# Three tables give the 1262 tasks of an attention and feed-forward kernel another order, other engines and other buffers

## The chip, the core and the metric

The kernel runs on one core of a Trainium2 chip. The time is device microseconds (us) of one execution, the median of three runs. The engines that the document speaks of are PE (the matrix engine), DVE (VectorE), ACT (ScalarE), POOL (GpSimd) and the DMA queue of SP (SyncE). PSUM is what PE writes its products into; SBUF is the working memory. All engines run at once, each through its own list of instructions in order.

## The reference

```python
def attention(q, k, v):            # B=4, H=8, S=768, D=64
    scores = q @ k.T / sqrt(D)     # heads 0, 2, 6: causal
    ...                            # heads 1, 3, 4, 5, 7: causal, and only the first
                                   # 4 keys and the last 64
    return softmax(scores) @ v

x = attention(q, k, v)  as 3072 tokens x 512
g = x @ w_gate                     # 512 x 1536
silu = g * sigmoid(g)
out = (silu * (x @ w_val)) @ w_out # 1536 x 512
```

Inputs and outputs are 32-bit floats. The kernel computes in 16-bit floats and sums in 32 bits.

## The kernel before

The 3072 tokens are 24 tiles of 128, and six groups g0 to g5 of four tiles. The attention goes by tiles t0 to t23. For a tile, q and k come from DRAM, are cast to 16 bits (the buffer ring `hq`) and transposed on PE. `sc` tasks (L571) are the score products, 64 rows deep; ACT takes their exponential (`exps`, L583, into the ring `e`); a `mask` task (L591) multiplies the exponentials by zeros and ones; PE multiplies by the values (L601); a `norm` task on DVE (`nm`, L608 and L609) divides by the row sums; PE transposes (L625), which gives the columns of the group's `xt`.

The feed-forward goes by groups. For g0 and g1, gate and value products are plain (L763), 12 pieces of 128 hidden columns each. ACT takes the tanh (L769), DVE makes silu from it (`stt1`, L776) and multiplies by the value product (`stt2`, L790, into `h_sb`). From g2 on the value product, and for g4 and g5 the gate product too, is made from seven half-size block products (`w_product`, L1092) instead of eight. These need sums of weight blocks (`vw`, L1041) and of `xt` blocks (`xs`, L1072), copies of partial results from PSUM into SBUF (`wy`, L211 on ACT, L213 on DVE, into the ring `raw`), additions (`wa` and `wb`, L1113), silu on ACT (L1134), and the product of gate and value (`wh`, L1151 on POOL, L1154 on DVE, into `h_sb`). The output product of every group is made from seven block products as well (`seventh`, L845, tasks `out0.p1` to `out5.p7`). It needs sums of blocks of `h_sb` (`hs`, L815; `hs4.2.0` is sum 2 of group 4, first half) and of the output weights (`ws`, L416). Its seventh product p3 needs sum 4. The results are gathered in `out_sb` (`oe`, L889 and L213) and stored by a DMA.

Rings are small sets of buffers. `raw` has 11 buffers of 4 KB a partition, and serves loads, the `wy` copies and some sums; `e` has 6, `xb` 3, `sil` 3. PSUM has 8 `banks`. A task that takes a buffer waits until the last users of the one that stood in it are done. At the very start ACT (or DVE) fills the mask patterns (`mfill`, L288) once.

All this is written as tasks: each has a name, the engines it may run on, what it depends on, and the rings it takes from. Nothing decides the order at build time but three tables of numbers. `ORDER` is a list of 1262 two-character numbers in base 62: the sequence in which the tasks are emitted, and each engine and each DMA queue runs its own tasks in that sequence. `WAYS` has a digit for each task: which of its possible engines runs it. `SLOTS` has a digit for each buffer that is taken: which buffer of the ring, or which PSUM bank. Two lines give the choices that the prediction speaks of most: a copy or sum has its engine from the table, and `wh` on POOL is another instruction than `wh` on DVE.

```python
ENG[T_hs[g, x][part].way].tensor_tensor(out=to, in0=a, in1=b, op=op)   # hsum, L815
...
if T_wh[g, s, name].way == "POOL":
    nc.gpsimd.tensor_tensor(out=to, in0=w_cell("g", g, s, name),
                            in1=w_value("v", g, s, name), op=ALU.mult)
```

Of the kernel before, what the change touches and what calls it, by code (L numbers as in the profile page):

```python
# [21 lines left out]
    "3Z3f9h0l443G459j493g4A3a9k9l9q3n463c1F3H0L0r0K0M3h9r9m3o3dA73A3p3B3q3r9b9c3zA23e1G4H47A8A3A94N4K"
    "AA3sA54L4O4C4Q4R4DA4AB3t4ZA6AF484BAE4Y8eAG3w3xAHAkBJAnAl0N0u184e0P0v0O4g0x4f0s0SAmAoBEBM4E4FBTBH"
    "4dBKBL4M3y5DBFBO4GBNBGAzBWB9BU4cBV5CBPBIBQBXB04bBA4V8f4P8g4i4lBCAu4I1H1Q5g0t5K4hB14j1BBBBDAx4S4T"
    "Af4mAv12Aw8hAaB2Ai0w5L0R5J5n5I5o4WAgAy4UAh4q4oBR15Ab1E4r4p4v1K1I4n4aB3AjAcAp514yAq524z4k1M1R4sBS"
    "4tAr4u1S1O1JACAD545W5T555U5X5f5350AI1N8kAJB4AK5M56AO5Y8l1LAMAPAN0T0W0b4J4w57Ad580Q5H5E6M1P1T5h6L"
    "5G6K7P5N5k5FB55i0U6H6J5j59AQAs5AAeAR5cALAUB74x5l4X5BAtB6B8AVAS5v5V5OBb8iBw5p5s5w5qAW0V5m0X0Y5tCF"
    "C0BxAXC1C75P5QBz5RC8CG6IATCUCMC2CbCVDBCW5Z5aCHC3Cc6v8jBy5r5uCdC45b5dCXC5CYCB5x6wC9606O6P6N735S74"
    "CZAZCI72CNCC5yCaC6CQCDCeDCCJCKCA5z66CfCE67DJDFDK63CRCgDDDEBaBcCO64DG686165CSCLCP6EChD76RCTDLDMCi"
    "6SD8DHDID9DABY7F697G6ACvCwCz6Z6UCj6aBZD06B6CBdBeCxCy6D6eBfCk6VBg7C6XBk6YAY620a5e0d6Q0Z7H6TClCmD1"  # L30
    "DRD37DD4DS7L7O6W7E6zBiBlBh6FD2D5DTBm6y80Bn706G0e7X717WBj81Dt6bDN6cCrBoDOCsD66dDU6xCtDPCu6p6hBqBp"
    "6q6i6f7I7J7KBrCnCoDvDuDQCp0c7U896gERES6k75BsDxET6l766mBtCqDy6n7bDzE46oE07c776jE5DXDYE678EgE16rEU"
    "E26s79E3EVEY6tFK7A7QEhE7EZ7eEW7fDZEiEj7YDaEaDw0f857j88827BBu866u87Bv7N7VFLEcEdFMFOEwEeEkEXFP7Z7a"
    "EfFQElEb7RF0ECE8FNEmFR8m7T7d7M7SExEDF1EnE9EyEzF2EJF8DVDcDbEAEKELENEEF4F3EB7g7hDWF5EFF97iDd7mEGDh"
    "F67nEHF7Di7pEo7k7qEpEODeFAFBEPEIEMEQDjDk8oDg7x8q84EqEr8A8B7rFq8s7o8C8nDf7s8D8N837tDlDm8Q8R8YEsFC"
    "7u7v8Z8E7wDn8I8GDoFG8pFr8F8SFDEtEuEv7yFH8J8HDpG8GFFIFEFJFFG9FuGaGAGh8KGGFvGbDqFs8rFVG18L8MGiGjG2"
# [1332 lines left out]
```

## Time and profile before

| what | before |
|---|---|
| time, median of 3 runs | 237.11 us (236.71 to 237.15) |
| profiled execution, its time | 236.62 us |
| its span | 234.8 us |
| PE busy | 224.4 us, 96% |
| DVE busy | 208.3 us, 89% |
| ACT busy | 177.6 us, 76% |
| POOL busy | 162.9 us, 69% |
| granted clock of PE, mean | 0.998 |

The span goes from the first to the last instruction of the profiled execution; its time has 1.8 us more around it. The granted clock is in parts of the higher of PE's two levels, 2.4 GHz. A busy share is a mean over stages that are limited by different things.

### The profile page before, as it was taken

To read this page: it belongs to the slowest core of one execution; us is meant where nothing else is said; L and a number is where in the kernel's file an instruction comes from. 1 tells how busy PE (TensorE), PEld (TensorE's weight loads), DVE (VectorE), ACT (ScalarE), POOL (GpSimd) and SP (SyncE) were. 2 spreads that over 40 slices of the span, in tenths; PEclk is the share of its full clock that TensorE was granted. 3 is DMA by queue.
4 is the path that set the end of the run, shared out by engine and by line. 5 is a ranking of instruction groups with operands and counts; after the bars stand their busy time and mean duration, and the time that the engine had idled before them with its cause. 6 is when DMAs were issued, how large, how long until landed. Compare 5 with 4: busy or idle time off the path is not lost.

```text
span 234.8 us, 6223 instructions
## 1 busy us (share of the span) xinstructions
PE 224.4 (96%) x2418; PEld 165.9 (71%) x2418; DVE 208.3 (89%) x373; ACT 177.6 (76%) x294; POOL 162.9 (69%) x180
## 2 busy tenths in 40 slices
...
GB/s 177 334 360 349 349 366 330 310 255 271 323 324 145 286 203 250 153 170 209 209 170 145 112 139 178 4 0 25 24 146 80 3 0 92 41 49 3 36 147 179
DMA packets 67197, 40.77 MB, mean 174 GB/s; under 512 B 25184, under 2 KB 61024, under 8 KB 67168
## 3 DMA queue, kind: packets, MB, share of 16 engines
...
## 4 chain that ended last, share of the span: by engine, by line
PE 76%; DVE 11%; SPq 4%; issue 3%; DMA 2%; POOL 1%; ACT 1%; DVEq 0%; POOLq 0%; ACTq 0%
PE banks L845 23%; PE banks L1092 20%; PE banks L763 20%; PE banks L571 6%; PE banks L601 5%; SPq L353 3%; DMA raw<-in_k_dram 2%; DVE h_sb L790 2%; DVE sil L776 2%; DVE e L591 2%; POOL h_sb L1151 1%; PE banks L477 1%; SPq L358 1%; DVE xb L609 1%; DVE h_sb L1154 1%
## 5 line engine op out<-in xcount | busy, mean ns | idle before, releaser
L583 ACT ACTIVATE e<-banks 128x1024 f16<-128x1024 f32 (+2 forms) x68 | 59.6, 914 | 9.4 <-PE banks L571 8.4
L763 PE MATMUL banks<-xt,wg_sb 128*128 128x512 f16 (+1 forms) x208 | 48.4, 363 | 0.8 <-DVE h_sb L790 0.7
L211 ACT COPY raw<-banks 128x512 f32<-128x512 f32 x61 | 33.9, 589 | 17.8 <-PE banks L1092 8.9
L845 PEld LDWEIGHTS <-h_sb 128*128 128x128 f16 x420 | 40.4, 98 | 7.0 <-issue 0.4
L769 ACT ACTIVATE sig<-banks 128x512 f32<-128x512 f32 (+1 forms) x52 | 28.6, 567 | 6.4 <-PE banks L763 3.7
L763 PEld LDWEIGHTS <-wg_sb 128*128 128x128 f16 x208 | 18.7, 98 | 16.7 <-issue 1.2
L1113 DVE TENSOR_TENSOR raw<-banks,raw 128x512 f32<-128x512 f32 x36 | 24.0, 684 | 3.7 <-ACT raw L211 2.1
L815 POOL TENSOR_TENSOR h_sb<-h_sb 128x768 f16<-128x768 f16 x11 | 18.7, 1707 | 12.2 <-DVE hs_sb L815 7.2
L845 PE MATMUL banks<-wt_sb,h_sb 128*128 128x256 f16 x216 | 26.2, 273 | 0.0
L591 POOL TENSOR_TENSOR e<-e,m 128x640 f16<-128x640 f16 (+1 forms) x14 | 24.8, 1779 | 0.9 <-ACT e L583 0.6
L845 PE MATMUL banks<-wo_sb,h_sb 128*128 128x256 f16 x204 | 24.9, 273 | 0.3 <-DVE h_sb L790 0.3
L763 PE MATMUL banks<-xt,wv_sb 128*128 128x512 f16 (+1 forms) x112 | 24.6, 349 | 0.0
L213 POOL CAST vt<-raw 64x512 f16<-64x512 f32 x24 | 14.8, 620 | 13.1 <-DMA raw<-in_v_dram 12.3
L571 PEld LDWEIGHTS <-kT 64*128 64x128 f16 x472 | 14.5, 94 | 11.0 <-issue 10.0
L571 PE MATMUL banks<-qT,kT 64*128 64x128 f16 x472 | 21.2, 218 | 0.4 <-DVE kT L213 0.2
L1092 PE MATMUL banks<-raw 128*128 128x256 f16 x144 | 20.3, 273 | 0.6 <-ACT raw L211 0.6
L1092 PEld LDWEIGHTS <-raw 128*128 128x128 f16 x192 | 18.1, 98 | 3.8 <-issue 0.8
L601 PEld LDWEIGHTS <-e 128*128 128x128 f16 x472 | 17.6, 97 | 4.3 <-issue 1.1
L1113 POOL TENSOR_TENSOR raw<-raw 128x512 f32<-128x512 f32 x12 | 16.0, 1331 | 6.4 <-DVE raw L213 3.7
L601 PE MATMUL banks<-vt,e 128*128 128x65 f16 x472 | 18.8, 193 | 1.2 <-POOL vt L213 0.8
L609 DVE TENSOR_TENSOR xb<-banks,rc 128x512 f16<-128x512 f32 x24 | 16.6, 691 | 0.8
L776 DVE SCALAR_TENSOR_TENSOR sil<-sig,banks 128x512 f32<-128x512 f32 (+1 forms) x28 | 16.6, 606 | 0.5
...
## 6 DMA issues: line engine op xcount, KB each, us to landing
...
```

Of the source, the lines that this page charges most:

```text
L211: nc.scalar.copy(out=dst, in_=src)
L571: nc.tensor.matmul(sc[:, c:c + n, :], weights, moving, start=first, stop=last)
L583: nc.scalar.activation(out=to, in_=src, func=AF.Exp, scale=scale)
L591: ENG[task().way].tensor_tensor(out=ev, in0=ev, in1=mm, op=ALU.mult)
L601: nc.tensor.matmul(avs[t][:, odd, n * 66:n * 66 + 65], ee, vv, start=(m == 0), stop=(m == len(bl) - 1))
L609: nc.vector.tensor_tensor(out=xb.rearrange("p n o d -> p o n d"), in0=av[:, :, :, 0:64], in1=rc.to_broadcast([128, 2, 4, 64]), op=ALU.mult)
L763: nc.tensor.matmul(ps, wsb[:, kk, j * 128:(j + 1) * 128], xt[:, kk, c[0]:c[1]], start=(kk == 0), stop=(kk == 3))
L769: nc.scalar.activation(out=sg[g, j, c], in_=gs[g, j, c], func=AF.Tanh, scale=0.5)
L776: nc.vector.scalar_tensor_tensor(out=sl[g, j, c], in0=sg.pop((g, j, c)), scalar=1.0, op0=ALU.add, in1=gs.pop((g, j, c)), op1=ALU.mult)
L845: nc.tensor.matmul(rooms[g, p][:, x, lo:hi], left[:, j, 128 * x:128 * x + 128], right[:, j, lo:hi], start=(on is None and (j == 0 if apart ...
L1092: nc.tensor.matmul(w_rooms[on][:, m], right, left[:, kk], start=(begins and m == 0 and kk == 0), stop=(kk == 1), skip_group_check=True)
L1113: ENG[T_wc[mat, g, s, name].way].tensor_tensor(out=to, in0=other, in1=to, op=ALU.add)
```

## The change

The three tables are replaced. The 1262 tasks, their dependencies and the instructions that each engine form of a task issues are the same. About 170 tasks run on another engine than before, the emitting sequence differs nearly throughout, and buffers and banks are dealt anew. The packed work of each engine stays nearly what it was: the moves between DVE, ACT and POOL go both ways. The first lines of each table:

```diff
 ORDER = (
-    "0607090A08000201202122231Z1Y1b0B251a0C0D041U1V0h0n0G0g0m0E0k1W031c1d1X1f1g1i051j1e1h281p2B1r2W2X"
...
 WAYS = (
-    "000011000000000000000000000000000000000000000000000000000000012002202212202102021010000110010110"
...
+    "000010000000000000000000000000000000000000000000000000000000212022122202222201021010011011101020"
...
 SLOTS = (
-    "65879104218319647A8636400543570374730564275A9835971023532245002212163406011042020206340121372062"
...
+    "034201675A127053142756590A7125769265938984809A6390A467520634362314120602436062414034402031523461"
```

What the tables do is seen in the engines' lists. The first place is the start, ACT. `mfill` fills are the rows at L288 (m_101 to m_103 are mask patterns), the casts to `hq` are the first halves of q and k, and the first row at L583 is the exponential of tile 0. Before:

```order
L288 ACT_TABLE_LOAD
L288 ACTIVATE m_101<-nat 128x256 x2
L288 ACTIVATE m_101<-nat 128x384
L288 ACTIVATE m_101<-nat 128x128
L288 ACTIVATE m_103<-nat 128x384
L288 ACTIVATE m_103<-nat 128x128
L288 ACTIVATE m_102<-nat 128x256
L211 CAST hq<-raw 128x2x4x64 x2
L288 ACTIVATE m_103<-nat 128x128
L288 ACTIVATE m_102<-nat 128x256
L583 ACTIVATE e<-banks 128x1024 x6
```

The same place with the change:

```order
L211 ACT_TABLE_LOAD
L211 CAST hq<-raw 128x2x4x64 x2
L288 ACTIVATE m_101<-nat 128x256 x2
L288 ACTIVATE m_101<-nat 128x384
L288 ACTIVATE m_101<-nat 128x128
L288 ACTIVATE m_103<-nat 128x384
L288 ACTIVATE m_103<-nat 128x128
L288 ACTIVATE m_102<-nat 128x256
L211 COPY kT_104<-banks 128x512
L583 ACTIVATE e<-banks 128x1024 x2
```

The casts moved ahead of the fills; a copy of kT came to ACT ahead of the first exponential; the last two fills went to DVE.

The second place is the end of the stage in which attention tiles 9 to 11 run beside g0's feed-forward. On DVE the rows from the masks (L591) to the sum of value weights (L1041) stand around tile 10; `wt_sb` rows (L416) are `ws` sums. Before, from the mask of tile 10 on:

```order
L591 TENSOR_TENSOR e<-e,m_102 128x1024
L416 TENSOR_TENSOR wt_sb<-wo_sb 128x512
L416 TENSOR_TENSOR wt_sb<-wo_sb,wt_sb 128x512
L790 SCALAR_TENSOR_TENSOR h_sb<-sil,banks 128x512
L776 SCALAR_TENSOR_TENSOR sil<-sig,banks 128x512
L608 RECIPROCAL rc<-banks 128x8
L609 TENSOR_TENSOR xb<-banks,rc 128x2x4x64
```

With the change:

```order
L591 TENSOR_TENSOR e<-e,m_102 128x1024
L591 TENSOR_TENSOR e<-e,m_103 128x640
L416 TENSOR_TENSOR wt_sb<-wo_sb 128x512
L1041 TENSOR_TENSOR raw<-wv_sb 128x768
L776 SCALAR_TENSOR_TENSOR sil<-sig,banks 128x512 x2
L608 RECIPROCAL rc<-banks 128x8
L609 TENSOR_TENSOR xb<-banks,rc 128x2x4x64
```

The second mask of tile 10 and a weight sum came to DVE, one `ws` sum left. POOL at the same place before (`wo_sb` casts are output weights, `vt` casts values, `hq` casts q and k; m_103 is the pattern of the second mask of a tile):

```order
L213 CAST wo_sb<-raw 128x1024
L416 TENSOR_TENSOR wt_sb<-wo_sb 128x512
L213 CAST hq<-raw 128x2x8x64
L416 TENSOR_TENSOR wt_sb<-wo_sb 128x512 x2
L591 TENSOR_TENSOR e<-e,m_103 128x640
L213 CAST vt_110<-raw 64x2x2x2x64
L213 CAST hq<-raw 128x2x8x64
L213 CAST vt_109<-raw 64x2x2x2x64 x3
```

With the change:

```order
L815 TENSOR_TENSOR h_sb<-h_sb 128x3x256
L1041 TENSOR_TENSOR raw<-wv_sb,raw 128x768
L213 CAST wo_sb<-raw 128x1024
L416 TENSOR_TENSOR wt_sb<-wo_sb 128x512
L213 CAST wo_sb<-raw 128x1024 x2
L416 TENSOR_TENSOR wt_sb<-wo_sb 128x512 x2
L416 TENSOR_TENSOR wt_sb<-wo_sb,wt_sb 128x512 x2
L416 TENSOR_TENSOR wt_sb<-wo_sb 128x512
L815 TENSOR_TENSOR h_sb<-h_sb 128x3x256
```

The mask and the casts of q, k and v are no longer between the weight sums; casts and sums of weights, and `hs` sums, stand there one behind the other.

The third place is POOL from group 4's last `wh` tasks on. The rows at L1151 are `wh4.2.c11` alone and then `wh4.2.c22`, `wh4.2.c12` before; L815 into `h_sb` ahead of them are sums of group 3, L815 into `hs_sb` is `hs4.1.1`, and the two L815 rows behind it are `hs4.4.0` and `hs4.4.1`:

```order
L1151 TENSOR_TENSOR h_sb<-raw 128x2x256
L1072 TENSOR_TENSOR raw<-xt 128x512
L815 TENSOR_TENSOR h_sb<-h_sb 128x3x256 x2
L1113 TENSOR_TENSOR raw<-raw 128x512
L1151 TENSOR_TENSOR h_sb<-raw 128x2x256 x2
L1113 TENSOR_TENSOR raw<-raw 128x512
L815 TENSOR_TENSOR hs_sb<-h_sb 128x768
L815 TENSOR_TENSOR h_sb<-h_sb 128x3x256
L1113 TENSOR_TENSOR raw<-raw 128x512
L815 TENSOR_TENSOR h_sb<-h_sb 128x3x256
```

With the change the first three L1151 are `wh4.1.c11`, `wh4.1.c22`, `wh4.2.c11`; L815 into `hs_sb` are `hs4.1.0` and `hs4.1.1`; the two L1151 between them are `wh4.2.c22` and `wh5.0.c11`; the L815 rows behind are `hs4.3.1`, `hs4.2.1`, `hs4.2.0` and, last, `hs4.4.1`:

```order
L1151 TENSOR_TENSOR h_sb<-raw 128x2x256 x3
L1072 TENSOR_TENSOR raw<-xt,raw 128x512
L1072 TENSOR_TENSOR raw<-xt 128x512
L815 TENSOR_TENSOR hs_sb<-h_sb 128x768
L1151 TENSOR_TENSOR h_sb<-raw 128x2x256 x2
L815 TENSOR_TENSOR hs_sb<-h_sb 128x768
L815 TENSOR_TENSOR h_sb<-h_sb 128x3x256
L815 TENSOR_TENSOR h_sb<-hs_sb,h_sb 128x3x256 x2
L1113 TENSOR_TENSOR raw<-raw 128x512 x2
L1151 TENSOR_TENSOR h_sb<-raw 128x2x256
L1113 TENSOR_TENSOR raw<-raw 128x512
L1151 TENSOR_TENSOR h_sb<-raw 128x2x256
```

`wh4.2.c12` went to DVE, the sums of group 3 went to DVE, three sums of group 4 came from DVE to POOL, and `hs4.4.0` went the other way. The row of `hs4.4.1` follows directly behind this piece.

## Rows read from the trace of the kernel before

**Rows 1.** The page: busy time by engine, and the last chain by engine.

```profile
PE 224.4 (96%) x2418; PEld 165.9 (71%) x2418; DVE 208.3 (89%) x373; ACT 177.6 (76%) x294; POOL 162.9 (69%) x180
...
PE 76%; DVE 11%; SPq 4%; issue 3%; DMA 2%; POOL 1%; ACT 1%; DVEq 0%; POOLq 0%; ACTq 0%
```

**Rows 2.** PE's timeline: start, us, instruction, [idle before, who ended it].

```profile
60.64 1.02 PE L763 MATMUL banks<-xt,wg_sb 128*128 128x512 f16 x4 [0.74 <-DVE h_sb L790]
73.86 0.93 PE L601 MATMUL banks<-vt,e 128*128 128x65 f16 x25 [0.28 <-DVE e L591]
75.13 1.47 PE L845 MATMUL banks<-wo_sb,h_sb 128*128 128x256 f16 x12 [0.34 <-DVE h_sb L790]
...
200.81 1.19 PE L1092 MATMUL banks<-xt,wv_sb 128*128 128x256 f16 x8 [0.83 <-DVE raw L213]
203.47 0.60 PE L1092 MATMUL banks<-raw 128*128 128x256 f16 x4 [0.59 <-ACT raw L211]
```

**Rows 3.** The chain of waits, 77 to 82 us: start, us, what.

```profile
78.34 1.31 PE banks L845 x12
...
80.20 1.42 PE banks L845 x12
```

**Rows 4.** ACT's timeline at the start.

```profile
4.33 2.25 ACT L288 ACTIVATE m<-nat 128x256 f16<-128x256 f16 x7 [2.30 <-POOL nat L264]
6.48 1.12 ACT L211 CAST hq<-raw 128x512 f16<-128x512 f32 x2
...
9.32 1.02 ACT L583 ACTIVATE e<-banks 128x1024 f16<-128x1024 f32 x1 [1.19 <-PE banks L571]
```

**Rows 5.** DVE's timeline: three long instructions, and a mask of the usual length.

```profile
57.08 2.06 DVE L591 TENSOR_TENSOR e<-e,m 128x1024 f16<-128x1024 f16 x1
67.59 1.40 DVE L1041 TENSOR_TENSOR raw<-wv_sb,raw 128x768 f16<-128x768 f16 x1
72.74 1.07 DVE L591 TENSOR_TENSOR e<-e,m 128x1024 f16<-128x1024 f16 x1
...
90.00 0.68 DVE L591 TENSOR_TENSOR e<-e,m 128x1024 f16<-128x1024 f16 x1
```

**Rows 6.** Groups by line and shape, DVE: busy, mean ns, idle before.

```profile
L1041 DVE TENSOR_TENSOR vt<-wg_sb,kT 128x768 f16<-128x768 f16 x2 | 1.1, 550 | 0.0
```

**Rows 7.** POOL's timeline at the middle place.

```profile
56.96 1.65 POOL L1041 TENSOR_TENSOR raw<-wv_sb 128x768 f16<-128x768 f16 x1
...
83.45 0.61 POOL L213 CAST vt<-raw 64x512 f16<-64x512 f32 x1 [10.19 <-DMA raw<-in_v_dram]
```

**Rows 8.** Windows: PE, PEld, DVE, ACT, POOL busy (counts), clock, DMA share, GB/s.

```profile
60.00:70.00 10.00, 9.36 (x76) 4.69 (x76) 9.65 (x15) 8.95 (x14) 8.57 (x10) 1.00 1.14 331
```

**Rows 9.** The chain of waits, 196 to 203 us.

```profile
196.92 0.54 ACT raw L1134
...
197.53 2.52 POOL h_sb L1151 x2
...
200.08 0.59 ACT raw L211
...
200.68 2.06 DVE h_sb L1154 x2
```

**Rows 10.** DVE's and POOL's timelines, 200 to 203 us.

```profile
201.27 1.45 DVE L1154 SCALAR_TENSOR_TENSOR h_sb<-raw 128x512 f16<-128x512 f32 x1
200.90 1.27 POOL L1113 TENSOR_TENSOR raw<-raw 128x512 f32<-128x512 f32 x1 [0.87 <-DVE raw L213]
```

**Rows 11.** The tail: the window from 206 us, POOL's timeline, PE's.

```profile
206.00:231.60 25.60, 25.57 (x235) 22.68 (x232) 21.18 (x36) 10.84 (x21) 13.17 (x9) 1.00 0.19 66
...
209.06 1.64 POOL L815 TENSOR_TENSOR h_sb<-h_sb 128x768 f16<-128x768 f16 x1 [4.83 <-DVE h_sb L1154]
211.88 1.65 POOL L815 TENSOR_TENSOR h_sb<-h_sb 128x768 f16<-128x768 f16 x1
...
219.19 2.78 PE L845 MATMUL banks<-wo_sb,h_sb 128*128 128x256 f16 x24
```

More of the change, by code (lines that the diff above doesn't have):

```diff
@@ L22 @@
[L22 to L36, printed above, removed]
@@ new lines @@
+    "0J0o0I0p9Y9d353S3T193E3Q173u3F369e9Z399vA0379w9fA19a3v3l3W9n0l0M0r0P0K0L3m3X3i3U9o9p2T3f9i3V3j3Y"
+    "3Z439g40443a3g3H41459h1A3k3h3c9b3n469l3o429j3d3A9q3e471G1F3G9cA7494A4Z9k3B9m9r3p4H3qA24K3rA8A9A3"
+    "3sA5AA3tA4A6AB4LAu4C4N4Q3y4D4MAF488eBJ4OAvAxAwBKBLAy4Y5D4B3w0u4g0N5L0x4R185KAkB9BMAl0O0t0v4e0s4h"
+    "0S4f4P4dAE1H1S3zAH8g1BBNAmBOAn3x4EBTBP4bBAAoBQBB4FBC4GAz5CBU4VB04cBDBV1Q15121I1K1R0w5I0W5J0Q0R4J"
+    "B1BWBEBFBX4o4l4i4p4j4aBHAfBG4IBI4vAg4mAp4S4TB2BRAq4W5g1EAh4UB3ArBSAi514y4q4r52AaAbB4B54zAj4k4n1M"
@@ new lines @@
+    "8fAc1N1O4s4tACB64u501PAG1J545T5WAIAJAD6J5H5UAKAdAsAOAM4w555f5X5FAPALAeAt8i531T1L5YAN8h0X5n0U4x5l"
+    "0b565M570T4X6M585NAQ5G6KAR6L5O59B75c5AB8AU5v5s5pAS5VAV5w5t5q5B0V6H5E5m0Y5o5j5kBw7P60ATAW5P5Q5ZCF"
+    "CUCMAX5RC7C0Cb8jBx5r8kBy5uBz8l6v5h5iCGCVCNCHCWDB5aC1CcCXC86ICYCfC25d5b5x5yDCC3CZCaC4CgChCB6wC5CI"
+    "5z66CdCOC967726N5S6P7374CCCiDDC6CJCD63CQCKCeCL64CACP61Bb6EBd6568DFCECRCS696RD7DGDECTDHDIDJCz6SD8"
+    "6A7F6ZD9DKD06a7GDACvDR6B7C6CDLD1CwDSDMD2DTCx6DCyBYDNAZ7D6X6UAY710a7O0Z625e0e6G6O6Q0dBZ6Y6V6FDO6T"
@@ new lines @@
+    "BaBg7HBcBeBfDU6zD3DPBkCrD46yCsD5DQD66W7LBj6bCj6cBq817E6f70DtDuCkBl6e6xBmBnCtBh6dClCu6p6h6iCnCmBr"
+    "Dx7I7J7KCo806qDyBo756k766lBpBiCpBsDzERE0Cq887U7W0f6g7N0c6n7bE4DvDX6jBt6m8mDZE5777cEYE1EgESE2ET6o"
+    "E378796r6s827ADwE6EZEUEh7R6tEwEV7Y7eE7Ei7TEjEW7f7Z8nEa84F0EXEcEJE8ECF1EbDY7X7B87897VBv6u86BuEdF2"
+    "EkFKEeExEyF3E985ElEmEzFLEAF4F8EnFMF5F6Ef7a7SDVEDEKF9EEEF7MFAEBFBFNF7ENFOEoEpEqEGDdEHFPDW7dDa7Q8q"
+    "DcELEI7g7hEM7jDbEODe7iDh7m7pEPDiDjFQErDgEQ7xDf8o7n7qDk7s8D8ADl7t8BDmFRFC8p8s7o7rFDFE8C7kFqFr8N8Y"
@@ new lines @@
+    "8QDn8Z7u7v8E838R8FDo7wFGEsFHFI8I8GDpFt7yFJFF8J8HDqEtEu8rFuGhGaFv8tFsGbGFFw8KG8GiG9G1GGG2EvFx8L8M"
+    "GcGAFy8T8WFzGdGB8UG4GeGf8XGCGkG5GlGDG0G6GIGmGEGoGvGgFVGJGK8SG3GHGjHIHOHKFXGnHJ7lDr7zDs8PHGG7GpHM"
+    "GwHLGLHHFSFZHNFUFWFY8VHUFaGqGrGMGyGTGsGNGOH2H9GtFTGUFeGzH3FbHA8OGVGuGxHBFfHP8aFk8bH0H4HQHSHRHTH5"
+    "GP8cH1HVGQGWH6FgHCGRH7HYHZ8dFdFcGXHDI2FhI3FlGSH8GYHWHXHEIDI6I7HFGZImInHaI5I4HgHbFmI8IoFiFnI9IpIE"
+    "HcHdIFIAIqIBIGItIuJUIKIwIRICIHIIILJSIrIMJ0IUIsHiIvFjIxIyJVFoHeISIzJTJ1FpINHhHjHlHkJ7IOIPHfIJJ8J2"
```

55 lines of the change are left out of this document (25 added, 30 removed).

## The prediction

> **What bounds the kernel now.** I read the page first, for busy time and for the last chain: PE works 224.4 of 234.8 us, DVE 208.3, and the chain that ended last is 76% PE and 11% DVE [rows 1]. So the end moves in two ways only: PE is given less to do, or one of its pauses goes or comes. The change has the same tasks, so the first way is nearly shut, and I went through PE's timeline for pauses behind another engine. Behind the start there are two places where PE waits in earnest [rows 2]. The reader is to see who ends each wait. In the middle, 60 to 75 us, it is DVE three times: 0.74 + 0.28 + 0.34 = 1.36 us. Late, at 200 to 204 us, it is a copy from PSUM to `raw`, once on DVE and once on ACT: 0.83 + 0.59 = 1.42 us. Then I read, for each place, the timelines of DVE and POOL and the chain of waits, to see why the releaser was late.
>
> In the middle DVE is full (9.65 of 10 us) while POOL works 8.57 [rows 8]. Three DVE instructions are much longer than their like [rows 5, 6]: a mask 2.06 us where another took 0.68, a sum of value weights 1.40 where 0.55 is usual, another mask 1.07. All three have two inputs in SBUF, and the first lies over a POOL sum that began at 56.96 and took 1.65 us [rows 7]. The excess is 1.38 + 0.85 + 0.39 = 2.62 us. That is more than the 1.36 us PE waits, so without the holds DVE would have been in time. Instructions of DVE that read one operand from PSUM keep their length over the same POOL work.
>
> Late, the chain of waits reads backward like this [rows 9]: PE's second pause ends with an ACT copy at 202.83, which needs a `raw` buffer that two DVE products (`wh5.0`) free; they need 2.06 us, because one of them is 1.45 us long beside a POOL addition [rows 10]. They stood behind a DVE copy that, like the ACT copy at 200.08, waited for a `raw` buffer; that buffer was freed by `wh4.2.c22` and `wh4.2.c12`, both on POOL, 2.52 us from 197.53 [rows 9]. These waited for ACT's silu at 196.92 and stood one behind the other.
>
> **The change part by part.** The sum is made against the profiled execution (236.62 us, span 234.8 and 1.8 around it); it is 0.49 below the median of 237.11, and I carry the difference over to the median.
>
> *PE's own work.* The same matmuls run. A row of output products behind score products took 1.42 us and one behind other work 1.31 [rows 3], so each entry into the 64-row scores costs about 0.1 us (an estimate from this pair). In the order of PE's list the scores stand in 36 separate groups before and 35 with the change: 0.1 us less; between 0 and −0.2.
>
> *Start.* Before, the fills (2.25 us) come first on ACT, then the casts (1.12), and the first exponential begins at 9.32 [rows 4]. With the change the casts come first, which lets PE begin earlier, but 2.25 us of fills and a copy then stand between the casts and the first exponential: I get it at about 10.1, 0.8 later. In exchange the second tile's q and k come earlier and ACT has less left after. PE's work up to the first gate product is limited by loads and DVE as well, so I put 0; bounds −0.4 (PE starts that much earlier and keeps it) and +0.8 (the whole delay of the exponential reaches PE).
>
> *Middle.* DVE's two-input instructions from 52 us to the last of the three waits are 7 before and 8 with the change: the second mask of tile 10 and a sum of value weights come, one sum of output weights goes. POOL's list there loses the mask and the casts of q, k and v that wait for loads (it waited 10.19 us for one [rows 7]) and becomes a row of casts and sums of weights without a pause. Nothing here tells which instructions will meet, since which of the two starts first decides. Per instruction the excess before was 2.62 / 7 = 0.37; eight of them make 3.0, so +0.4 us, which goes through to PE since DVE has no slack here. Lower bound: nothing is held and the 1.36 us of waits go, −1.4. Upper bound: five of eight held by the mean of the three long ones, 2.62 / 3 = 0.87, make 4.35, so +1.7.
>
> Read beside this: the Trainium skill, "SBUF — State Buffer", section "Who interferes with whom", says that DVE and GpSimd share one pair of ports as an exclusive lock, that a DVE instruction with two SBUF inputs contends with a GpSimd instruction that reads SBUF, and that the one issued first keeps it for its whole length. Rows 5 and 7 agree. By the rule, with POOL busy 0.86 of the stretch, nearly every one of the eight would meet an occupied port; half a POOL instruction of 1.2 us each makes about 0.5 x 8 = 4.1 us, an estimate, and the sum would come out 1.1 us higher than mine, 237.5 us. What hangs on it is the first rival, which is priced from rows alone.
>
> *Late.* `wh4.2.c12` leaves POOL for DVE, so that it no longer stands behind `wh4.2.c22`; the two group 3 sums and the addition that stood ahead of them on POOL are gone; and more PE work stands between the product that the late copies follow and the one that needs them. Each of these alone gives the copy at 200.08 its buffer about 1.3 us earlier (one POOL product of the pair that takes 2.52), enough for the pause of 0.83; the second pause of 0.59 hung on the first, through DVE's list. So −1.4. On DVE `wh4.2.c12` costs 0.68 us or 1.45 when held [rows 10]; behind it in DVE's list are additions of the same group that free PSUM banks, and DVE waited for POOL here before, so there is room. Bound: 0, if the buffers are dealt so that the wait stands elsewhere.
>
> *Tail.* From 206 us on PE has no pause (25.57 of 25.60 busy) and POOL works only 13.17 [rows 11]. POOL then waited 4.83 us before `hs4.4.0` and ended `hs4.4.1` at 211.88 + 1.65 = 213.53, 5.7 us ahead of the output product at 219.19 that needs both [rows 11]. The change gives POOL, from `hs4.1.1` to `hs4.4.1`, five sums of 1.65 us and five products or additions of 1.27 [rows 10, 11]: 14.6 us without a pause, so from about 202.1 to 216.7, while the output product comes 1.4 earlier, at 217.8. That leaves 1.1 us, in which every hold by DVE and every wait for an input has to fit. I take +0.4 (one hold of the size above and a little waiting use up 1.5 of the 1.1); bounds 0 and +1.5.
>
> The sum: −0.1 + 0 + 0.4 − 1.4 + 0.4 = −0.7 us. The profiled execution would take 235.9 us and the median 236.4.
>
> **The rivals.** *First, on the other side: DVE is held by POOL in the middle.* One mechanism, one place: at 52 to 77 us, five or more of the eight two-input instructions meet a POOL instruction. Then the middle term is +1.7 instead of +0.4, and the sum −0.1 + 1.7 − 1.4 + 0.4 = +0.6, a time of 237.7; with six held 238.6. It decides from an excess of about 3.7 us on (4.2 for a change that can be measured), against 2.62 now. For it: POOL's uninterrupted row of sums there, and DVE's 9.65 of 10 us. Against it: of seven only three were held, with POOL just as busy.
>
> *Second: the late wait only moves.* The eleven `raw` buffers are dealt anew, and the gaps between a copy and its reader are a few tenths there. If half of the 1.42 us returns at another product of g5, the sum is −0.1 + 0.4 − 0.7 + 0.4 = 0: 237.1. For it: DVE now has `wh4.2.c12` and the sums of group 3, ahead of copies that PE needs. Against: three things that made the wait are gone at once.
>
> *Third: the start is late.* The exponential's 0.8 us goes through, sum +0.1: 237.2. For it: nothing on ACT hides the fills any longer. Against: PE gets its first work earlier.
>
> *Fourth: more is won than I put.* No long hold in the middle and room in the tail: −0.1 − 1.4 − 1.4 = −2.9 at most, half of it likelier, 235.2.
>
> **How the numbers follow.** Forecast (late wait gone, the rest evens out, 235.6 to 236.6) 0.38; first rival 0.27; second 0.16; third 0.09; fourth 0.10. A difference under 0.2% (0.47 us) can hardly be told from none here. Faster: forecast and fourth, 0.48. Same: second and third, 0.25. Slower: the first, 0.27. The likeliest case gives 236.4. The range goes from 235.0 (half of the fourth case is below) to 238.2 (the first rival's five held, 237.7, and half of the way to six); some 0.15 lies outside.
>
> **What would show it.** Late: no wait of PE above 0.3 us between 196 and 205 us, and `wh4.2` on two engines. Middle: count DVE's masks and weight sums over 0.9 us between 50 and 78 us, and add what they have over 0.68 or 0.55; PE's waits behind DVE there should sum to about 1.8. Start: first exponential near 10.1, first gate product within 0.4 of where it was. Tail: `hs4.4.1` ending within 1.5 us of the output product that needs it, with a wait of a few tenths at the most. The forecast is wrong if the excess in the middle is above 3.7 us, if a wait for a `raw` buffer stands elsewhere after 195 us, or if PE waits for a sum on POOL at 210 to 222 us by more than 1 us.

## The result, and the profile after

The changed kernel takes 233.42 us (233.23 to 233.67), the kernel before 237.13 in the same comparison: a ratio of 0.9849 [0.9826, 0.9872], 3.7 us faster. The forecast was 236.4 with a range from 235.0 to 238.2. The sign was right, the size was not, and 233.42 lies outside the range. The profiled executions took 233.35 and 236.62 us. Medians and ratios leave out executions that took over 1.5% more than the fastest of the same kernel (one with the other kernel's order on SP, three with the early cast of k8).

The page of the changed kernel, busy time by engine; it answers to [rows 1]:

```profile
span 231.6 us, 6221 instructions
PE 223.0 (96%) x2418; PEld 165.6 (71%) x2418; DVE 205.4 (89%) x381; ACT 178.9 (77%) x295; POOL 160.3 (69%) x171
```

The matmuls are the same 2418. Of the 3.2 us between the spans, 1.8 are idle time of PE (8.6 instead of 10.4) and 1.4 its busy time, in which pauses can hide, since the ends of matmuls are modelled. Windows of the changed kernel (us, busy PE, PEld, DVE, ACT, POOL with counts, granted clock, DMA share, GB/s) at the two places of the prediction; they answer to [rows 2, 8]:

```profile
60.00:70.00 10.00, 10.00 (x96) 5.25 (x93) 9.70 (x20) 8.45 (x16) 9.78 (x9) 1.00 1.12 336
70.00:80.00 10.00, 10.00 (x116) 6.53 (x115) 9.76 (x20) 9.90 (x14) 6.27 (x6) 1.00 1.21 250
80.00:90.00 10.00, 10.00 (x142) 8.30 (x140) 9.84 (x22) 9.60 (x15) 6.81 (x9) 1.00 1.21 214
90.00:100.00 10.00, 10.00 (x116) 8.24 (x114) 9.79 (x21) 9.87 (x17) 6.14 (x8) 1.00 1.00 172
...
200.00:210.00 10.00, 10.00 (x94) 8.96 (x93) 7.92 (x14) 5.89 (x11) 8.27 (x6) 1.00 0.01 2
```

PE is busy for the whole 10 us in each of them; before it had 9.36 of 10 from 60 to 70 us [rows 8]. Of the five pauses in [rows 2] none is left. PE's timeline of the changed kernel has one pause above 0.3 us between 25 us and the last stage (0.35 at 32.69), and this one in the last stage:

```profile
214.64 1.47 PE L845 MATMUL banks<-wo_sb,h_sb 128*128 128x256 f16 x12
...
223.83 1.47 PE L845 MATMUL banks<-wt_sb,hs_sb 128*128 128x256 f16 x12 [0.29 <-DVE out_sb L889]
```

To see where time went although the tasks come in another order, I made an account from the two traces: for each PE task the time from its start to the next task's start, less the median of its kind over both traces, added up in order of time. It counts what PE lost, shown as a pause or not, and pauses come out larger than their rows (0.83 as 0.99, 0.59 as 0.75), for the same reason.

| change of the account from before to after | us |
|---|---|
| up to 50 us | +0.6 |
| 50 to 80 us | -2.1 |
| 80 to 100 us | -0.2 |
| 100 to 190 us, many small ones | -0.6 |
| 190 to 210 us | -1.9 |
| 210 us to the last product | +0.5 |
| sum | -3.7 |

Behind the last product 0.4 us more pass (3.6 instead of 3.3 to the end of the span), which makes, to rounding, the 3.2 us between the spans.

DVE in the middle of the changed kernel, two-input instructions; they answer to [rows 5, 6]:

```profile
52.91 0.69 DVE L591 TENSOR_TENSOR e<-e,m 128x1024 f16<-128x1024 f16 x1
54.58 0.56 DVE L1041 TENSOR_TENSOR raw<-wv_sb 128x768 f16<-128x768 f16 x1
...
72.32 1.14 DVE L591 TENSOR_TENSOR e<-e,m 128x1024 f16<-128x1024 f16 x2
73.72 0.55 DVE L1041 TENSOR_TENSOR raw<-wv_sb 128x768 f16<-128x768 f16 x1
```

All have their usual length (two masks of 0.68 and 0.48 in 1.14). None of DVE's ten such instructions from 52 to 77 us was held by 0.1 us or more. One reason is DVE's own list: from 55.2 to 72.3 us, where POOL works nearly without a pause (9.78 of 10 us in the window above), it has none of the ten. Before, the two longest stood in that stretch, at 57.08 and 67.59 [rows 5]. POOL's timeline gives the other reason; it answers to [rows 7]:

```profile
54.73 1.66 POOL L591 TENSOR_TENSOR e<-e,m 128x640 f16<-128x640 f16 x1 [3.23 <-ACT e L583]
73.94 1.35 POOL L416 TENSOR_TENSOR wt_sb<-wo_sb,wt_sb 128x512 f16<-128x512 f16 x1 [1.43 <-DVE wt_sb L416]
```

POOL stood still for 3.23 us, waiting for an exponential, while DVE did its masks at 52.9 to 54.7; and for 1.43 us, waiting for a sum on DVE itself, while DVE did its row at 72.3 to 73.7.

### The profile page after: what moved, and what is told of

It reads as the page before. It is cut to its first block, busy times and chain, and to the rows that moved or that the text cites. A ratio compares the mean times of both kernels' runs of the same rounds, so it can differ in the third digit from the quotient of the medians.

```text
span 231.6 us, 6221 instructions
## 1 busy us (share of the span) xinstructions
PE 223.0 (96%) x2418; PEld 165.6 (71%) x2418; DVE 205.4 (89%) x381; ACT 178.9 (77%) x295; POOL 160.3 (69%) x171
## 5 line engine op out<-in xcount | busy, mean ns | idle before, releaser
L583 ACT ACTIVATE e<-banks 128x1024 f16<-128x1024 f32 (+2 forms) x68 | 59.7, 913 | 3.7 <-PE banks L571 2.2
L763 PE MATMUL banks<-xt,wg_sb 128*128 128x512 f16 (+1 forms) x208 | 47.8, 363 | 0.1
L211 ACT COPY raw<-banks 128x512 f32<-128x512 f32 x62 | 34.6, 594 | 16.8 <-PE banks L1092 13.1
L591 POOL TENSOR_TENSOR e<-e,m 128x1024 f16<-128x1024 f16 (+1 forms) x17 | 30.5, 1800 | 8.7 <-ACT e L583 8.6
L1113 POOL TENSOR_TENSOR raw<-raw 128x512 f32<-128x512 f32 x13 | 17.0, 1325 | 15.5 <-ACT raw L211 9.7
L763 PE MATMUL banks<-xt,wv_sb 128*128 128x512 f16 (+1 forms) x112 | 24.1, 349 | 0.0
L1151 POOL TENSOR_TENSOR h_sb<-raw 128x512 f16<-128x512 f32 x10 | 12.9, 1297 | 13.5 <-DVE raw L1113 6.0
L776 DVE SCALAR_TENSOR_TENSOR banks<-sig,banks 128x512 f32<-128x512 f32 x24 | 16.1, 689 | 1.3 <-ACT sig L769 0.9
L790 DVE SCALAR_TENSOR_TENSOR h_sb<-sil,banks 128x512 f16<-128x512 f32 (+1 forms) x28 | 16.5, 606 | 0.7 <-PE banks L763 0.4
```

The lines of the kernel that those rows point to most:

```text
L211: nc.scalar.copy(out=dst, in_=src)
L583: nc.scalar.activation(out=to, in_=src, func=AF.Exp, scale=scale)
L591: ENG[task().way].tensor_tensor(out=ev, in0=ev, in1=mm, op=ALU.mult)
L763: nc.tensor.matmul(ps, wsb[:, kk, j * 128:(j + 1) * 128], xt[:, kk, c[0]:c[1]], start=(kk == 0), stop=(kk == 3))
L790: nc.vector.scalar_tensor_tensor(out=hs[g, j][:, c[0]:c[1]], in0=sl.pop((g, j, c)), scalar=1.0 if g in SILU else 0.5, op0=ALU.mult, in1=vs ...
L1113: ENG[T_wc[mat, g, s, name].way].tensor_tensor(out=to, in0=other, in1=to, op=ALU.add)
```

## The experiments

**One product from POOL to DVE.** `wh4.2.c12` in the kernel before, at its place in the sequence:

```diff
 WAYS, the digit of wh4.2.c12
-1
+0
```

> The kernel before, with one digit of WAYS changed: wh4.2.c12 runs on DVE instead of POOL, at the same place of the sequence. Theory A (the late waits come from the two products that stand one behind the other on POOL): the raw buffer is free some 1.2 us earlier, PE's waits of 0.83 and 0.59 us at 200 to 204 us go, and the time falls by 1.0 to 1.8 us, to 235.3 to 236.1. Rival B (the silu that both wait for, and the group 3 sums ahead of them, make the waits as much): less than 0.6 us is won.

Measured: 234.87 us against 237.04, ratio 0.9899 [0.9877, 0.9922]. PE's timeline has no pause between 190 and 210 us. POOL's and DVE's timelines of this run; they answer to [rows 9, 10]:

```profile
197.30 1.35 POOL L1151 TENSOR_TENSOR h_sb<-raw 128x512 f16<-128x512 f32 x1 [1.27 <-ACT raw L1134]
```

```profile
196.83 0.68 DVE L1154 SCALAR_TENSOR_TENSOR h_sb<-raw 128x512 f16<-128x512 f32 x1
...
199.28 0.68 DVE L1154 SCALAR_TENSOR_TENSOR h_sb<-raw,banks 128x512 f16<-128x512 f32 x1
199.88 0.68 DVE L1154 SCALAR_TENSOR_TENSOR h_sb<-raw 128x512 f16<-128x512 f32 x1
```

The product took 0.68 us on DVE, which in the kernel before waited 1.74 us for POOL up to 200.07; and the later product that POOL had held (1.45 us in [rows 10]) took 0.68. Theory A holds, with more than the 1.8 us at the end of its range: one digit is worth 2.2 us in the kernel before.

**The same product back on POOL in the changed kernel.**

```diff
 POOL
-L1151 TENSOR_TENSOR h_sb<-raw 128x2x256 x2
+L1151 TENSOR_TENSOR h_sb<-raw 128x2x256 x3
```

> The changed kernel with wh4.2.c12 back on POOL, directly behind wh4.2.c22, as it stood before. Theory A (the engine of this one product makes the late wait): 0.8 to 1.9 us slower, 234.2 to 235.3, with PE waits of 0.5 us or more at 195 to 203 us. Rival B (in the changed kernel POOL waits 3.10 us ahead of its next product there, since the group 3 sums are gone and the silu comes earlier, so that the second product has room on POOL): within 0.4 us of 233.42, no new wait.

Measured: 233.75 us, ratio to before 0.9875 [0.9851, 0.99], and no pause of PE at 190 to 206 us. Rival B holds. In the changed kernel the silu and the list ahead come so early that the pair began at 193.08 instead of 197.53 [rows 9]. The late wait had more than one way out, and the change took two at once.

**Two holds removed from the kernel before.** Each row moved one place earlier on DVE:

```diff
 DVE
-L776 SCALAR_TENSOR_TENSOR sil<-sig,banks 128x512
-L591 TENSOR_TENSOR e<-e,m_102 128x1024
+L591 TENSOR_TENSOR e<-e,m_102 128x1024
+L776 SCALAR_TENSOR_TENSOR sil<-sig,banks 128x512
...
-L776 SCALAR_TENSOR_TENSOR sil<-sig,banks 128x512
 L1041 TENSOR_TENSOR raw<-wv_sb,raw 128x768
+L776 SCALAR_TENSOR_TENSOR sil<-sig,banks 128x512
```

> The kernel before, with two rows of DVE's list moved one place earlier and nothing else: the mask of tile 9 (2.06 us in the trace of before) goes ahead of the stt1 at 56.48, and the sum of value weights (1.40 us) ahead of the stt1 at 66.99, so that each starts before the POOL instruction that lay over it. Theory A (which of the two starts first decides, and DVE's holds make PE's waits in the middle): the two have 0.68 and 0.55 us, DVE has 2.2 us back, PE's waits of 0.74, 0.28 and 0.34 shrink to 0.4 or less in sum, and the time falls by 0.9 to 1.7 us, to 235.4 to 236.2. Rival B (DVE's amount of work and its order make the waits, the holds are a symptom): within 0.4 us of before. Rival C (a hold spared here comes back on another pair): other masks or sums are long instead, within 0.5 us.

Measured: 237.69 us (236.39 to 239.48), ratio 1.0028 [0.9999, 1.0057]. DVE, PE and POOL of this run:

```profile
57.58 0.74 DVE L591 TENSOR_TENSOR e<-e,m 128x1024 f16<-128x1024 f16 x1
66.93 0.89 DVE L1041 TENSOR_TENSOR raw<-wv_sb,raw 128x768 f16<-128x768 f16 x1
```

```profile
89.17 0.38 PE L845 MATMUL banks<-wt_sb,h_sb 128*128 128x256 f16 x2 [1.62 <-POOL wt_sb L416]
90.28 1.03 PE L845 MATMUL banks<-wt_sb,h_sb 128*128 128x256 f16 x8 [0.73 <-POOL wt_sb L416]
```

```profile
85.95 1.93 POOL L213 CAST vt<-raw 64x512 f16<-64x512 f32 x3 [11.34 <-DMA raw<-in_v_dram]
87.97 2.26 POOL L416 TENSOR_TENSOR wt_sb<-wo_sb,wt_sb 128x512 f16<-128x512 f16 x2
```

The mask took 0.74 instead of 2.06, the sum 0.89 instead of 1.40, and PE's three pauses of the middle are gone. The mechanism is as theory A has it; the time did not fall. PE now came early to a product that needs two weight sums, and those stood on POOL behind casts that wait for a load.

**A third move: those sums ahead of the casts, on POOL.**

```diff
 POOL
-L213 CAST vt_109<-raw 64x2x2x2x64 x3
 L416 TENSOR_TENSOR wt_sb<-wo_sb,wt_sb 128x512 x2
-L213 CAST vt_109<-raw 64x2x2x2x64 x3
+L213 CAST vt_109<-raw 64x2x2x2x64 x6
```

> The kernel before with the two moves of the run with two moved rows on DVE, and a third: the output-weight sums ws4.1 and ws4.2 stand on POOL ahead of the six casts of values that wait for loads, instead of between them. In that earlier run the three waits of the middle were gone, but PE then waited 1.62 and 0.73 us at 87 to 91 us for ws4.1 and ws4.2, which stood behind casts that waited 11.34 us for a load. Theory A (the middle has two obstacles one behind the other: holds of DVE, then these sums behind the loads): PE has no wait above 0.5 us between 55 and 95 us, and the time falls by 1.0 to 1.7 us, to 235.4 to 236.1. Rival B (the loads or SP's queue pace the whole stage to 90 us, so that time won before them is always lost at them): a wait of a similar sum stands at another product, and the time is within 0.5 us of before.

Measured: 237.12 us against 237.07, ratio 1.0005 [0.9981, 1.003]. PE ran on to 90 us, with 1.5 us won by the account, and lost them right behind. PE and ACT of this run:

```profile
93.82 0.60 PE L1092 MATMUL banks<-xt,wv_sb 128*128 128x256 f16 x4 [1.03 <-ACT out_sb L211]
97.63 1.03 PE L1092 MATMUL banks<-raw 128*128 128x256 f16 x8 [0.56 <-ACT raw L211]
```

```profile
92.24 1.04 ACT L211 CAST hq<-raw 128x1024 f16<-128x1024 f32 x1 [1.48 <-DMA raw<-in_k_dram]
95.92 1.04 ACT L211 CAST hq<-raw 128x1024 f16<-128x1024 f32 x1 [0.69 <-DMA raw<-in_q_dram]
```

Copies that PE needs stood on ACT behind casts that wait for loads. With `wh4.2.c12` on DVE as well:

> The kernel before with the three moves of the run before this one and, as the fourth edit, wh4.2.c12 on DVE (which alone gave 234.87 us against 237.04). Theory A (the changed kernel's gain is these two places and nothing else of size): the gains add, 2.2 late and 1.0 to 1.7 in the middle, so 233.2 to 233.9, as fast as the changed kernel (233.42). Rival B (the middle is paced by loads): 234.5 to 235.2, only the late gain.

Measured: 235.26 us, ratio 0.9927 [0.9901, 0.9952]. No more than the late gain: rival B, 0.06 us above its range.

**A fourth move: the load of k8 earlier on SP.**

```diff
 SP
 L358 DMA raw<-in_q_dram 128x8x128
+L358 DMA raw<-in_k_dram 128x8x128
 L619 DMA_TRANSPOSE xt<-xb 128x4x128
 L467 DMA_TRANSPOSE qT_107<-hq 128x8x64
 L619 DMA_TRANSPOSE xt<-xb 128x4x128 x2
-L358 DMA raw<-in_k_dram 128x8x128
```

> The kernel before with the three moves (two on DVE, the two weight sums on POOL) and one more, on SP's queue: the load of k8 is issued ahead of the transposing DMA xdma10, some 7 us earlier, instead of behind xdma11. With the three moves alone PE lost the time it had won in the middle at 92 to 98 us: ACT's cast of k8 waited 1.48 us for that load, and copies that PE needs stood behind it; SP issued without a pause up to there. Theory A (the third obstacle is this cast that waits for its load): ACT no longer waits there, PE's wait of 1.03 us at 93.8 goes, and the time is 0.6 to 1.2 us below the three moves alone (237.12), 235.9 to 236.5. Rival B (SP's queue is what paces the stage, so a load that comes earlier makes the transposes behind it later by 0.6 us each): within 0.4 us of the three moves.

> The same five edits on the kernel before: the four of the run above, and wh4.2.c12 on DVE (2.2 us by itself). Theory A: 233.6 to 234.3, close to the changed kernel (233.42). Rival B: 234.7 to 235.3, as with the three moves and that digit (235.26).

Measured: 237.3 us, ratio 1.0016 [0.9995, 1.0037], and 235.44 us, ratio 0.993 [0.9906, 0.9955]. ACT's cast of k8 no longer waits, but a transposing DMA behind the load on SP came late, and PE waited for that. At its new place the issue of the load took 2.57 us of SP's queue, at its old one 0.57, and the transposing DMA of q was issued at 85.73 instead of 83.61. PE of the first of the two (the second has the same wait, 1.41):

```profile
89.27 0.71 PE L571 MATMUL banks<-qT,kT 64*128 64x128 f16 x19 [1.41 <-DMA qT<-hq]
```

Rival B again, the second 0.14 us above its range. Three times what was won in the middle was lost at 85 to 98 us, each time to another transfer.

**A hold put into the changed kernel.** Two neighbours on POOL exchanged:

```diff
 POOL
-L416 TENSOR_TENSOR wt_sb<-wo_sb,wt_sb 128x512 x2
+L416 TENSOR_TENSOR wt_sb<-wo_sb,wt_sb 128x512
 L416 TENSOR_TENSOR wt_sb<-wo_sb 128x512
+L416 TENSOR_TENSOR wt_sb<-wo_sb,wt_sb 128x512
```

> The changed kernel with two neighbours on POOL exchanged: ws3.1, which waits for nothing, ahead of ws2.1, which waits 1.43 us for DVE at 72.5 us. POOL then works beside DVE's row of two-input instructions (mask10.0, mask10.1, ws1.1, vw1.1v), which no POOL instruction met in the changed kernel. Theory A (who starts first decides, and the changed kernel escaped the holds because POOL waited for DVE just there): one or two of the four are held, by 0.5 to 1.2 us together; PE's first waiting place behind it is tile 11's scores; the time grows by 0.2 to 0.9 us. Rival B: none is held, or PE has so much cover there that nothing reaches it: within 0.2 us.

Measured: 234.37 us (233.84 to 234.55), on the chip on which the run with the product back on POOL took 233.75 (233.52 to 234.45). DVE, POOL and PE of this run:

```profile
72.44 2.12 DVE L591 TENSOR_TENSOR e<-e,m 128x1024 f16<-128x1024 f16 x2
```

```profile
72.60 1.61 POOL L416 TENSOR_TENSOR wt_sb<-wo_sb 128x512 f16<-128x512 f16 x1
```

```profile
74.61 0.60 PE L601 MATMUL banks<-vt,e 128*128 128x65 f16 x14 [0.26 <-DVE e L591]
77.45 0.40 PE L571 MATMUL banks<-qT,kT 64*128 64x128 f16 x8 [0.38 <-DVE xb L609]
```

The two masks took 2.12 instead of 1.14 us and POOL's sum 1.61 instead of the 1.15 of its like. Each held the other in turn, and PE waited for DVE at two places behind. Theory A holds by these rows: PE's account is 1.0 us worse at 80 us than in the changed kernel, and the difference stays to the end, with spans of 232.7 and 231.6 us. The times say less, since the medians are 0.6 apart and the ranges overlap.

**The cast of k8 ahead of the copies in the changed kernel.**

```diff
 ACT
+L211 CAST hq<-raw 128x2x8x64
 L211 COPY raw<-banks 128x512 x7
-L211 CAST hq<-raw 128x2x8x64
```

> The changed kernel with one row of ACT's list moved: the cast of k8 stands ahead of the seven copies of g2's block products, as it stood ahead of most of them before, instead of behind them. The load of k8 is issued at 86.97 us in the trace of the changed kernel and lands some 5 us later, when the first copy has just run. Theory A (casts that wait for loads ahead of copies that PE needs are the obstacle that keeps a gain in the middle from arriving): PE waits 0.8 to 2 us at 90 to 97 us, and the time grows by as much, to 234.2 to 235.4. Rival B (PE has other work there): within 0.3 us of 233.42.

Measured: 235.89 us (234.87 to 238.37), ratio to before 0.9981 [0.9936, 1.0025], where another form of the changed kernel (the one with the last experiment's digit) took 233.22 on the same chip. ACT and PE, from an execution of 235.08:

```profile
92.10 1.04 ACT L211 CAST hq<-raw 128x1024 f16<-128x1024 f32 x1 [0.98 <-DMA raw<-in_k_dram]
93.06 3.51 ACT L211 COPY raw<-banks 128x512 f32<-128x512 f32 x7
```

```profile
93.68 1.08 PE L1092 MATMUL banks<-raw 128*128 128x256 f16 x8 [0.92 <-ACT raw L211]
```

In the profiled execution theory A fits, in size too. The times fall into two parts: with a granted clock of 0.999 or 1.0 three executions took 234.87 to 235.08 us, inside theory A's range, and with 0.990 to 0.992 four took 235.89 to 238.37. What the second part lost besides the wait is open, since none of these executions has a profile here.

**SP's order exchanged between the two kernels.** Thirteen rows of SP's queue in the other kernel's order, first in the kernel before with its three moves (then also with `wh4.2.c12` on DVE), with two buffers dealt anew, then in the changed kernel. The core of the first:

```diff
 SP
+L467 DMA_TRANSPOSE kT_104<-hq 128x8x64
 L363 DMA raw<-in_moe_w_out_dram 128x2x512
+L467 DMA_TRANSPOSE qT_106<-hq 128x8x64
+L358 DMA raw<-in_v_dram 128x8x128
+L467 DMA_TRANSPOSE qT_106<-hq 128x8x64
+L358 DMA raw<-in_v_dram 128x8x128
...
```

> The kernel before with the three moves (two on DVE, the two weight sums on POOL), and 13 rows of SP's queue, from the load of o4 to the load of q8 (63 to 80 us), in the order that the changed kernel gives them: the loads of x8 and x6 earlier, xdma8 earlier, three transposes of k later. DVE, ACT and POOL keep their lists. Theory A (SP's order in this stage paces PE from 85 to 98 us, and the changed kernel's order is what lets the gain of the middle through): 235.4 to 236.4 against 237.12 with the three moves alone. Rival B (ACT's and POOL's lists have to fit the loads, SP's order alone does not help): 236.8 or more.

> The same with wh4.2.c12 on DVE. Theory A: 233.3 to 234.3. Rival B: 234.8 or more (three moves and that digit: 235.26).

> The changed kernel with 13 rows of SP's queue, from the load of q9 to the last transpose of k7 (74 to 91 us), in the order of the kernel before: the load of q9 goes from the first place to the last but one. ACT's list has the cast of q9 at 88.85 us, ahead of seven copies of g2's block products. Theory A (what counts is whether the data of a cast has landed when its engine comes to it): the cast waits until about 95 us, PE waits 2 to 5 us behind the copies, and the time is 235.5 to 239. Rival B: PE has other work, within 0.5 us of 233.42.

Measured: 241.2 us (ratio to before 1.0184 [1.0153, 1.0216]), 240.45 (1.0164 [1.0109, 1.0218]) and 239.94 (1.0126 [1.0058, 1.0195]). The second of the three, first PE, then POOL and DVE:

```profile
80.41 1.16 PE L845 MATMUL banks<-wt_sb,h_sb 128*128 128x256 f16 x9 [1.22 <-DVE h_sb L815]
84.89 1.47 PE L845 MATMUL banks<-wt_sb,h_sb 128*128 128x256 f16 x12 [1.61 <-DVE out_sb L213]
90.48 1.02 PE L763 MATMUL banks<-xt,wv_sb 128*128 128x512 f16 x4 [1.95 <-DVE out_sb L889]
```

```profile
76.63 1.08 POOL L213 CAST hq<-raw 128x1024 f16<-128x1024 f32 x1 [5.65 <-DMA raw<-in_q_dram]
78.61 2.75 POOL L416 TENSOR_TENSOR wt_sb<-wo_sb,wt_sb 128x512 f16<-128x512 f16 x2 [0.89 <-DVE wt_sb L416]
...
78.85 1.50 DVE L815 TENSOR_TENSOR h_sb<-hs_sb,h_sb 128x768 f16<-128x768 f16 x1
80.28 1.44 DVE L591 TENSOR_TENSOR e<-e,m 128x640 f16<-128x640 f16 x1
```

The third, first PE, then ACT and the windows behind the second wait:

```profile
88.84 0.73 PE L571 MATMUL banks<-qT,kT 64*128 64x128 f16 x19 [2.56 <-DMA qT<-hq]
98.31 1.72 PE L1092 MATMUL banks<-raw 128*128 128x256 f16 x8 [2.91 <-ACT raw L211]
```

```profile
95.45 1.04 ACT L211 CAST hq<-raw 128x1024 f16<-128x1024 f32 x1 [3.98 <-DMA raw<-in_q_dram]
...
95.00:98.00 3.00, 0.40 (x4) 0.20 (x3) 2.28 (x6) 2.51 (x4) 0.00 (x0) 1.00 0.59 144
98.00:102.00 4.00, 3.69 (x21) 2.18 (x21) 0.00 (x0) 4.00 (x9) 0.00 (x0) 0.57 0.49 87
```

For the two on the kernel before, rival B: the other kernel's order of SP alone makes it worse. In the second the holds are back. POOL's cast of q waited 5.65 us for its load, and the sums behind it met DVE's row: a sum of DVE took 1.50 us, a mask 1.44, and PE's first wait is for that sum. In the run with the same DVE, ACT and POOL lists but without the change on SP (235.26 us) the cast waited 1.41 us, the same sum took 0.56 and the same mask 0.49, and it was POOL that was held there: its two sums took 4.91 us instead of 2.75. So the time at which a load lands also decides which of the two engines is held.

For the third, theory A, 0.9 us above its range. The cast of q9 waited 3.98 us for its load, and PE waited 2.91 us for the copies behind it, both as forecast. Two things were in no theory: PE's other wait, 2.56 us for a transposing DMA of q (issued at 83.12 instead of 79.48), and the clock. After the 3 us in which PE worked 0.40, the granted clock was 0.57 from 98 to 102 us, so PE ran mostly at the lower of its two levels, 1.2 GHz, and the wait cost more than its row says.

In these three runs an order of loads served only the lists of ACT, DVE and POOL that it was made with.

**Half of one kernel, half of the other.** Cut at the first output product of group 1, with 36 or 29 buffers dealt anew:

```diff
 ORDER, WAYS and SLOTS of the kernel before up to out1.p1
-from there those of the kernel before
+from there those of the changed kernel
```

> A hybrid: the sequence, engines and buffers of the kernel before up to the first output product of group 1 (107 us in its trace), and from there those of the changed kernel (36 buffers dealt anew where they would have clashed). Theory A (the gain is two separate ones, in the middle and late): this has the late one alone, PE's accounts in the two traces differ there by -1.9 us late and +0.4 in the tail, so -1.5 and perhaps -0.3 of small ones: 235.2 to 235.9, with the three waits of the middle still there. Rival (the gain is one of the whole sequence, or comes from the first stage): less than 0.8 us is won, or new waits appear behind the cut.

> The opposite hybrid: the changed kernel up to the first output product of group 1 (109 us in its trace), and from there the sequence, engines and buffers of the kernel before (29 buffers dealt anew). Theory A: this has the gain of the middle alone, by PE's accounts -2.1 us up to 110 us (of which +0.5 before 55 us, -1.75 at 55 to 75, the rest in small waits behind): 234.7 to 235.5, with the late waits of before (1.4 us) back. Rival: less than 1 us is won, the first part is not worth it by itself.

Measured: 238.69 us (ratio 1.0061 [1.003, 1.0091]) and 244.97 (1.0354 [1.03, 1.0408]). As times both came out far above theory A, since the seam costs several us: by the account about 3.5 in the first and 8 to 9 in the second. Their stages still tell something. The first has no pause from 190 to 215 us. The second has, at 100 us, the account of the changed kernel (-2.0 against -2.1; before -0.4), and late this in PE's timeline:

```profile
208.68 1.19 PE L1092 MATMUL banks<-xt,wv_sb 128*128 128x256 f16 x8 [0.81 <-DVE raw L213]
211.34 0.60 PE L1092 MATMUL banks<-raw 128*128 128x256 f16 x4 [0.59 <-ACT raw L211]
```

These are the two late pauses of before [rows 2], to 0.02 us. Each place goes with its part of the tables.

**Banks of the last stage.** In the changed kernel `out5.p5` takes other banks:

```diff
 SLOTS, the digit of out5.p5
-4
+2
```

> The changed kernel with one digit of SLOTS changed: out5.p5 takes banks 2 and 3 instead of 4 and 5. In the changed kernel it waits 0.29 us (0.46 by start to start) at 223.8 us for bank 4, which a gathering on DVE frees that began at 223.10. Theory A (the bank alone makes the wait): the wait goes and the time falls by 0.3 to 0.45 us, to 233.0 to 233.1. Rival B (the gathering behind out5.p5 on DVE, or the stores, come no earlier, so that the end stays): within 0.15 us of 233.42.

> The changed kernel itself, on the chip of the next run, as its yardstick: 233.2 to 233.7.

> The changed kernel with out5.p5 in banks 2 and 3, again. Theory A (the bank alone made the last wait): 0.25 to 0.45 us below the changed kernel on the same chip. Rival B (what follows comes no earlier): within 0.15 us of it.

Measured: 233.22 us (232.41 to 234.26) in the first run; on one chip then 234.1 us (232.97 to 235.0) for the changed kernel and 233.19 (232.66 to 234.35) with the digit. So this chip gave the changed kernel a ratio to before of 0.9878 [0.9848, 0.9909], 2.8 us. The pause of 0.29 us is gone, in PE's timeline of the last run:

```profile
220.96 2.78 PE L845 MATMUL banks<-wt_sb,h_sb 128*128 128x256 f16 x24
223.58 1.47 PE L845 MATMUL banks<-wt_sb,hs_sb 128*128 128x256 f16 x12
```

The gap of 0.9 us between the medians is more than that pause can give. The executions of one kernel spread over 2 us, and the profile of the slowest of the changed kernel (235.0) shows where, in PE's timeline:

```profile
91.06 2.79 PE L1092 MATMUL banks<-xt,wv_sb 128*128 128x256 f16 x24 [0.61 <-DMA xt<-xb]
```

So the digit is worth the pause, some 0.3 us by the spans of two profiles without the pause at 91 us (231.6 and 231.3). It is the fastest version here, by no more than that.

## Why the prediction was right or wrong

**Late, -1.4: right in place and cause, too small.** Measured -2.2 for the one product by itself, -1.9 in the account. The size was read from idle time in the rows, which is less than what PE loses from start to start (1.42 against 1.74), and the hold of 0.77 us on DVE went too. That either of two things would have done was foreseen ("Each of these alone"), and two runs show it: the product's engine alone did it in the kernel before, and the rest alone in the changed one.

**Middle, +0.4: wrong, and the step that failed.** It is the sentence "Per instruction the excess before was 2.62 / 7 = 0.37; eight of them make 3.0". The measured excess is none, the end that was kept only as a bound, and PE's account from 50 to 80 us is -2.1, below even the -1.4 of that bound, which was read from idle rows. From +0.4 to -2.1 is 2.5 us, as much as the whole miss (-0.7 forecast, -3.2 between the spans); the other terms' errors cancel. The count of instructions says nothing of how many meet. I read POOL's list as "a row of casts and sums of weights without a pause", but in the stretch without a pause DVE has none of the eight, and around it two rows of POOL depend on ACT's exponential and on a sum of DVE's own row, and POOL waits for them just while DVE works. The dependencies stand in the program, and the order showed both sides. The exchange on POOL is the test: with the dependent sum one place later the hold was there, 1 us.

**What was missing: the second obstacle.** I took it that DVE's lateness goes "through to PE since DVE has no slack here", and so to the end. In the kernel before, 1.5 us won in the middle never arrived: three versions without the holds were no faster than before. A stage to 98 us stood behind, in which sums, casts and transposing DMAs wait for loads. In the changed kernel the middle counts: the 1 us of the exchange on POOL is still there at the end of the span. That this is so because its lists meet the loads better is argued and not shown. What the rows show is less idle time there. ACT's busy time by windows of the kernel before is 8.80 and 8.45 us:

```profile
80.00:90.00 10.00, 10.00 (x116) 7.52 (x112) 9.80 (x21) 8.80 (x14) 5.84 (x8) 1.00 1.21 215
90.00:100.00 10.00, 9.80 (x118) 8.38 (x116) 9.93 (x21) 8.45 (x14) 5.98 (x7) 1.00 1.31 206
```

Of the changed kernel it is 9.60 and 9.87, for 32 instructions instead of 28. One cast moved back costs some 1.5 us there (234.87 to 235.08 against 233.42). Which rows of SP, ACT and POOL together carry the middle's 1.5 us stays open: SP's order taken over from the other kernel did not, ACT's and POOL's were not tried by themselves, and the hybrids lose more at the seam.

**Start, 0: right.** The first exponential came at 9.86 (10.1 was said, 9.32 before), and the first gate product at 19.88 (20.28 before). Taken from instruction to instruction, the account is even at 20 and at 30 us; the +0.6 of its first line arises from 30 to 50 us, for which the prediction has no term. ACT's timeline, against [rows 4]:

```profile
7.24 2.25 ACT L288 ACTIVATE m<-nat 128x256 f16<-128x256 f16 x7
9.39 0.56 ACT L211 COPY kT<-banks 128x512 f16<-128x512 f16 x1
9.86 1.93 ACT L583 ACTIVATE e<-banks 128x1024 f16<-128x1024 f32 x2
```

**Tail, +0.4: right in size, but by luck.** `hs4.4.1` ended at 212.91 + 1.64 = 214.55, 0.09 us ahead of the product that needs it at 214.64; against [rows 11]:

```profile
212.91 1.64 POOL L815 TENSOR_TENSOR h_sb<-h_sb 128x768 f16<-128x768 f16 x1
```

No wait followed, so the margin was enough. It was foreseen as 1.1 us, with POOL's row from 202.1 us and the product at 217.8; the row began at 197.60 and the product at 214.64, both earlier. Some 0.4 of the 0.5 us were lost for a PSUM bank instead, which one digit of SLOTS mends. The 0.4 us behind the last product were in no term, and their cause is open.

**The sum.** The -0.1 for score groups can't be told from other small things. Of the other terms, +0.6 - 2.1 - 1.9 + 0.5 and 0.8 us of small pauses between the places make the -3.7 of the account. Even the fourth rival had only the sum of the bounds seen in idle rows, -2.9, and the small pauses in no term. (Half of it is -1.45, which gives 235.7 and not the 235.2 of the prediction.) The chance of faster, 0.48, was too low for what two separate places could give, and the first rival, at 0.27, had the middle's sign wrong.

**The rule of the Trainium skill**, in "SBUF — State Buffer", section "Who interferes with whom": an exclusive lock, kept by whichever was issued first. The run with the hold agrees (DVE 2.12 for 1.14, POOL 1.61 for 1.15), and so does its absence where POOL waits. What I had worked out from it, half a POOL instruction per DVE instruction, 237.5 us, is an average over chance meetings, and the meetings of a fixed program are not chance.
